# Linear attention into a gated MLP: the first k tile loaded uncast, slot 5 transposed by DMA

## The chip, the cores and the metric

The kernel runs on one core of a Trainium2 chip. The core has TensorE (PE: matmuls; its weight loads are listed apart as PEld), VectorE (DVE), ScalarE (ACT), GpSimd (POOL) and SyncE (SP). DMAs are issued by SP, ACT or POOL and carried out by 16 DMA engines. The metric is device time in microseconds; all times in this text are microseconds unless marked otherwise. Data sits in SBUF (128 partitions) and matmuls write to PSUM, which has eight banks of 128 x 512 float32.

## What is computed

The first half is a recurrence over time with a decay per head, the second half an MLP with h * cos(h):

```python
# q, k, v: (4, 8, 768, 64) float32; w_in (512, 2048), w_out (2048, 512)
gamma = 1.0 - 2.0 ** (-5.0 - np.arange(H))
scale = 1.0 / np.sqrt(D)
for t in range(S):
    state = gamma[None, :, None, None] * state + einsum('bhd,bhe->bhde', k[:, :, t], v[:, :, t])
    y[:, :, t] = scale * einsum('bhd,bhde->bhe', q[:, :, t], state)
x = y.transpose(0, 2, 1, 3).reshape(B * S, H * D)     # 3072 x 512
h = x @ w_in
out = (h * cos(h)) @ w_out                            # 3072 x 512, float32
```

## The kernel before, in words

**Slots and groups.** Time is cut into six chunks of 128 steps. A slot is one chunk of two batches (all eight heads): 12 slots, numbered in the order of `ORDER` (slots 0 and 1 are the first chunks of both batch pairs). Two slots make one group of 512 tokens for the MLP: six groups.

**A slot's attention.** q and k come in as float32 tiles `qf`, `kf`, are cast to bf16 (`qs`, `ks`; q times the decay from slot 2 on), and are transposed into `qkt`. In slots 0 and 1 the transposes are `tq`, `tk` (per half `u`), later `t`: PE transposes by a matmul against the identity (line 364) into a bank, and DVE or ACT copy the bank to `qkt` (`eq`, `ek`). From slot `DMA_T` on, two transposing DMAs per slot, issued by SP (line 353; `dt60` is q of slot 6, `dt61` its k), write `qkt` directly. Then come the scores (`a`, lines 392 and 402), their masks on DVE (`m`, line 411; two of slots 0 and 1 are split into a copy by ACT, `ms`, and a product by POOL, `ml`), and the output block `y` (lines 483 and 497) with the state update (`s`, line 511). From slot 4 on, `y` of a slot holds the scores of the next slot as well (`y4` computes the scores of slot 5), so it takes six banks. `yc` copies y to `xt` (the MLP's x), `sc` copies the state to bf16. v is cast to `vr` in slots 0 and 1 (`rv`) and scaled to `vs` (`cv`); `cq`, `ck` are the casts of q and k. The last digit is the half.

**The MLP.** `h2.6` is w_in's columns of f tiles 6 and 7 times the half group of slot 2 (line 614, eight matmuls of 256 columns); `f0.13` is f tile 13 times a full group (line 593, four matmuls of 512 columns). ACT computes the cosine of the bank (`cos...`, line 601) and DVE the product into `gt` (`mul...`, lines 605 and 622). `o2.3` is the last quarter of the second matmul for 128 tokens (line 638, four matmuls); when four quarters are done, ACT copies the bank (`oc2`) and SP stores it (line 650).

**What sets the order.** Up to slot 5 the order of every engine is decided by `Plan`, a list scheduler that runs when the kernel is built: each operation has engines that may do it, a cost, what it waits for, a rank, and tokens that it takes (banks, cosine buffers, the port that DVE and POOL share). `SHIFT` adds a number to each rank and `ON` narrows the engines; both are tables of fitted numbers. The plan decides order only; waits on the chip are semaphores for data and buffers. An engine carries out its list in order, so an operation that waits holds up all behind it. Where PE has nothing to do before 18 us, the plan puts in idle matmuls on zeros (`fill`, line 667), behind seven that stand ahead of it. Seven banks go round in a fixed order; one PSUM bank holds the state. After the plan a plain loop writes the rest: per step one `f` and one `o` unit, and a `y` block every eighth step; its first `o` unit is the one of group 1.

**Loads.** POOL issues a fixed list, in which the first load is k of slot 0 (line 284, into bf16 `ks`, so the DMA casts), then:

```python
LOADS = ["Q1", "K1", "v0", "v1", "w0A", "w0B", "w0b", "w1a", "w1b", "w2", "q2", "k2", "w3a", "v2", "w3b", "o0",
         "q3", "k3", "v3", "o1", "q4", "o2", "k4", "v4", "q5", "k5", "o3", "v5", "q6", "k6", "v6", "q7", "k7", "v7"]
```

A capital Q or K is a load that casts; q, k, v load float32 tiles; w and o are parts of w_in and w_out (they cast too; `o0` to `o3` are quarters of w_out). q of slot 0 is loaded by SP, and SP loads all slots from 8 on. SP's list is: q of slot 0, five small copies (`sw`), then stores, transposing DMAs and later loads.

Of the kernel before, what the change touches and what calls it, by code (L numbers as in the profile page):

```python
# [28 lines left out]
class Plan:  # L29
# [35 lines left out]
    def run(self, start, cold_until=0.0, look=0.0, fill=None, hold=""):  # L65
# [6 lines left out]
        t = 0.0  # L72
        while left:
            nxt = []
            for e in "SPADE":
                if free[e] > t:
                    nxt.append(free[e])
                    continue
                best = None
                soon = 1e9  # L80
                coming = []
                for op in left:
                    if e not in op["engines"]:
                        continue
                    r = self.ready(op)
                    if r is None:
                        continue
                    if r > t + 1e-9:
                        nxt.append(r)
                        coming.append((r, op["rank"]))  # L90
                        if op["rank"] < 20:
                            soon = min(soon, r)
                        continue
                    ok = True
                    for k, n in op["take"]:
                        tk = sorted(self.tokens[k])
                        n += op["spare"] if k == "bank" else 0
                        if len(tk) < n:
                            ok = False
                            continue  # L100

                        at = max(tk[n - 1] - 0.5, tk[n - 3]) if n > 5 else tk[n - 1]
                        if at > t + 1e-9:
                            nxt.append(at)
                            ok = False
                    if not ok:
                        continue
                    key = (op["rank"] + (0.5 if op["mode"] and op["mode"] != mode[0] else 0), op["n"])
                    if best is None or key < best[0]:
                        best = (key, op)  # L110
                if e == "E" and best and best[0][0] >= 1000 and soon < t + look:
                    best = None
                if e in hold and best:
                    c = best[1]["cost"]
                    c = c[e] if isinstance(c, dict) else c
                    c = c[0] if isinstance(c, tuple) else c
                    if any(r < t + 0.7 * c and k < best[0][0] - 8 for r, k in coming):
                        best = None
                if best is None:
                    if (e == "E" and fill and fill[0] <= t < fill[1] and soon > t + fill[2]  # L120
                            and min(self.tokens["bank"] or [1e9]) <= t):
                        self.add("E", fill[2], fill[3], (), 0, (), (), "full", name="fill")
                        self.ops[-1].update(eng=e, start=t, free=t + fill[2], done=t + fill[2],
                                            lat=0.0)
                        free[e] = t + fill[2]
                        mode[0] = "full"
                        nxt.append(free[e])
                    continue
                op = best[1]
                left.remove(op)  # L130
                c = op["cost"][e] if isinstance(op["cost"], dict) else op["cost"]
                busy, took = c if isinstance(c, tuple) else (c, c)
                if e == "E":
                    if t < cold_until:
                        busy, took = 2 * busy, 2 * took
                    if op["mode"] != mode[0]:
                        busy, took = busy + self.SWITCH, took + self.SWITCH
                        mode[0] = op["mode"]
                for k, n in op["take"]:
                    self.tokens[k].sort()  # L140
                    del self.tokens[k][:n]
                op.update(eng=e, start=t, free=t + busy, done=t + took, lat=self.LAT[e])
                free[e] = t + busy
                if op["mb"]:
                    self.dma = max(self.dma, t + busy + 1.6) + op["mb"] / op["rate"] + op["lag"]
                    op.update(done=self.dma + 0.9, lat=0.0)
                for k, n in op["give"]:
                    self.tokens[k] += [op["done"] + 0.052] * n
                nxt.append(free[e])
                nxt.append(op["done"] + op["lat"])  # L150
            later = [x for x in nxt if x > t + 1e-9]
            if left and not later:
                raise RuntimeError("the plan is stuck at %s: %s" % (t, [o["name"] for o in left][:9]))
            t = min(later) if later else t
# [12 lines left out]
HOLD = ""  # L167
# [6 lines left out]
def kernel(  # L174
# [170 lines left out]
    def conv_k(p, b, e):  # L345
        copy(e, kb(p)[:, b], kf[p % PRE][:, b])
# [654 lines left out]
```

## Time and profile before

| | |
|---|---|
| time, median of 3 runs (lowest to highest) | 208.82 (208.31 to 208.92) |
| span of the profiled execution, first to last instruction | 206.6 |
| the profiled execution's own time | not recorded beside its span; the median is 2.2 above the span |
| PE busy | 201.9 (98%), 2179 matmuls |
| DVE, ACT, POOL busy | 112.9, 115.1, 75.2 |
| chain that ended last | PE 93%, DMA 4% |
| granted TensorE clock | full (1.000) |

The page of the profile lists the busy time of each engine, the span in 40 slices (each digit is a busy share in tenths), the chain of work that ended last, and groups of instructions. The trace behind it answers questions: a timeline (start, length, engine, line, operation, output<-input, count), who waited for whom, and from which issue a DMA landed when. "Landing" is the time from issue to arrival. Landings used below are issue plus that time: k of slot 0 at 7.7, Q1 9.4, K1 11.3, v0 13.0, o0 32.6, k6 57.3, k7 61.8, v7 63.3.

### The profile page before, as it was taken

What the parts mean: (1) busy time and instruction counts of PE and PEld (TensorE: products, weight loads), DVE (VectorE), ACT (ScalarE), POOL (GpSimd) and SP (SyncE); (2) the same over time, 40 slices, a digit from 0 to 9 for tenths busy, and PEclk for the clock granted to TensorE, in tenths of its full rate; (3) what the DMA queues carried; (4) which work ended last, traced back from release to release, by engine and by line L of the source; (5) the groups of instructions that cost most, each with busy time, mean ns of one, the idle gap of its engine ahead of it and who ended that gap; (6) DMA issues with size and microseconds to landing.
All of it is one profiled execution on the core that took longest, in us unless ns stands there. A gap on an engine that the chain in (4) does not pass through costs nothing.

```text
span 206.6 us, 5235 instructions
## 1 busy us (share of the span) xinstructions
PE 201.9 (98%) x2179; PEld 108.9 (53%) x2179; DVE 112.9 (55%) x194; ACT 115.1 (56%) x193; POOL 75.2 (36%) x79
## 2 busy tenths in 40 slices
PE   7999999999999999999999999999999999999994
PEld 2547665868945545445445445445444444444442
DVE  5477899776787548338438438448442444444000
ACT  7566794859965357547547546554555553554120
POOL 8899989799985003305206105200000000000000
PEclk9999999999999999999999999999999999999999
DMA  6999999999999865886876975501101101110212
GB/s 117 172 264 201 304 242 322 252 333 278 341 332 190 199 156 150 206 210 155 190 183 157 144 198 147 156 0 56 53 1 51 51 3 51 51 51 0 105 52 102
DMA packets 59656, 32.15 MB, mean 156 GB/s; under 512 B 48752, under 2 KB 54128, under 8 KB 59632
## 3 DMA queue, kind: packets, MB, share of 16 engines
q0 software_dynamic: 15408, 15.47, 34.6%
q1 hardware_dynamic: 44080, 16.28, 31.7%
q8 instruction: 17, 0.28, 0.6%
q10 hardware_dynamic: 144, 0.07, 0.1%
q14 instruction: 7, 0.06, 0.1%
HBM read 27.26 MB, written 6.29 MB: 162 GB/s over the span
## 4 chain that ended last, share of the span: by engine, by line
PE 93%; DMA 4%; POOL 1%; issue 0%; DVE 0%; POOLq 0%; DVEq 0%
PE bank L638 39%; PE bank L593 30%; PE bank L614 10%; DMA kx<-in_k_dram 4%; PE bank L392 2%; PE bank L483 2%; PE bank L364 2%; PE bank L658 2%; PE st_ps L511 2%; PE bank L667 2%; PE bank L497 1%; POOL ks L284 1%; PE bank L434 1%; POOL qs L284 1%; PE bank L402 0%
## 5 line engine op out<-in xcount | busy, mean ns | idle before, releaser
L601 ACT ACTIVATE cosb<-bank,halfpi 128x512 bf16<-128x512 f32 x96 | 65.6, 689 | 54.1 <-PE bank L593 47.8
L638 PE MATMUL bank<-w_out_sb,gt 128*128 128x512 bf16 x368 | 91.0, 379 | 0.0
L605 DVE TENSOR_TENSOR gt<-bank,cosb 128x512 bf16<-128x512 f32 x72 | 49.1, 689 | 55.7 <-ACT cosb L601 55.7
L593 PE MATMUL bank<-xt,w_in_sb 128*128 128x512 bf16 x288 | 73.2, 379 | 0.0
L638 PEld LDWEIGHTS <-gt 128*128 128x128 bf16 x368 | 35.5, 98 | 42.3 <-DMA w_out_sb<-in_moe_w_out_dram 0.3
L593 PEld LDWEIGHTS <-w_in_sb 128*128 128x128 bf16 x288 | 27.5, 98 | 32.3
L327 POOL TENSOR_TENSOR qs<-qf,gq 128x512 bf16<-128x512 f32 x18 | 18.5, 1046 | 42.4 <-PE bank L483 32.0
L411 DVE TENSOR_TENSOR am<-bank,mask 128x512 bf16<-128x512 f32 x40 | 24.8, 681 | 3.5 <-PE bank L392 3.5
L316 ACT COPY ob<-bank 128x512 f32<-128x512 f32 (+1 forms) x24 | 14.0, 582 | 16.0 <-PE bank L638 13.9
L614 PE MATMUL bank<-xt,w_in_sb 128*128 128x256 bf16 x192 | 22.4, 273 | 0.0
L614 PEld LDWEIGHTS <-w_in_sb 128*128 128x128 bf16 x192 | 18.6, 98 | 3.3 <-DVE xt L318 0.3
L622 DVE TENSOR_TENSOR gt<-bank,cosb 128x512 bf16<-128x512 f32 x24 | 16.2, 689 | 5.6 <-ACT cosb L601 5.4
L316 ACT CAST xt<-bank 128x512 bf16<-128x512 f32 x21 | 11.4, 588 | 10.6 <-PE bank L483 10.5
L316 ACT CAST ks<-kf 128x512 bf16<-128x512 f32 x20 | 11.5, 623 | 1.9 <-DMA kf<-in_k_dram 1.9
L667 PE MATMUL bank<-zero 128*128 128x512 bf16 x35 | 11.2, 449 | 1.1 <-DVE halfpi L683 1.1
L483 PE MATMUL bank<-am,vs 64*64 64x128 bf16 (+1 forms) x320 | 10.3, 206 | 0.1
L334 POOL TENSOR_TENSOR vs<-vf,gk 128x512 bf16<-128x512 f32 x8 | 8.2, 1043 | 6.0 <-DMA vf<-in_v_dram 3.8
L284 POOL DMA_DIRECT2D vf<-in_v_dram x8 | 9.4, 1178 | 1.9 <-DVE vs L339 1.4
L339 POOL TENSOR_TENSOR vs<-vf,gk 128x512 bf16<-128x512 f32 x8 | 8.7, 1096 | 2.5 <-PE bank L483 1.3
L318 DVE CAST stb<-st_ps 128x512 bf16<-128x512 f32 x9 | 6.2, 689 | 3.4 <-PE st_ps L511 2.6
L483 PEld LDWEIGHTS <-vs 64*64 64x64 bf16 x320 | 7.8, 107 | 0.5 <-POOLq L531 0.2
L392 PE MATMUL bank<-qkt 64*64 64x128 bf16 (+1 forms) x320 | 7.9, 206 | 0.0
(66 smaller groups left out, 131.7 us busy)
## 6 DMA issues: line engine op xcount, KB each, us to landing
out_dram<-ob SPq DMA_DIRECT2D x23, 256.0 KB, 2.5
vf<-in_v_dram POOLq DMA_DIRECT2D x8, 512.0 KB, 11.7
qf<-in_q_dram POOLq DMA_DIRECT2D x6, 512.0 KB, 12.3
kf<-in_k_dram POOLq DMA_DIRECT2D x6, 512.0 KB, 12.1
w_out_sb<-in_moe_w_out_dram POOLq DMA_DIRECT2D x4, 512.0 KB, 14.1
qf<-in_q_dram SPq DMA_DIRECT2D x4, 512.0 KB, 4.8
w_in_sb<-in_moe_w_in_dram POOLq DMA_DIRECT2D x5, 256.0 KB, 8.5
kf<-in_k_dram SPq DMA_DIRECT2D x16, 64.0 KB, 3.1
```

Of the source, the lines that this page charges most:

```text
L284: eng.dma_start(out=t.rearrange("p b h d -> p (b h) d"), in_=src[ds(2 * bp, 2), :, ds(c * C, C), :].rearrange("b h t d -> t (b h) d"))
L316: nc.scalar.copy(out=out, in_=in_)
L327: ENG[e].tensor_tensor(out=qb(p)[:, b], in0=qf[p % PRE][:, b], in1=bc(gq, ORDER[p] % NC), op=ALU.mult)
L411: nc.vector.tensor_tensor(out=am[p % 2][b][u], in0=bank.rearrange("p (a t) -> p a t", a=HP), in1=(dec[:, b] if p < 2 else mask[second(p, 0 ...
L483: m = nc.tensor.matmul(held["yp", p][b][ts(j, 64), a, lo:], lhsT=vs[p % NB][ts(r, 64), b, h, :], rhs=am[p % 2][b][h // 4][ts(r, 64), h % 4 ...
L593: nc.tensor.matmul(bank, lhsT=w_in_sb[:, i, ts(f, 128)], rhs=xt[g % 2][:, i, :], start=(i == 0), stop=(i == KIN - 1))
L601: nc.scalar.activation(out=cb, in_=bank, func=AF.Sin, bias=halfpi)
L605: nc.vector.tensor_tensor(out=gt[g % 2][:, f, :], in0=bank, in1=cb, op=ALU.mult)
L614: nc.tensor.matmul(bank[:, ts(e, 256)], lhsT=w_in_sb[:, i, ts(f + e, 128)], rhs=xt[g % 2][:, i, ts(hf, 256)], start=(i == 0 and e == 0), s ...
L622: nc.vector.tensor_tensor(out=gt[g % 2][:, f : f + 2, ts(hf, 256)], in0=bank.rearrange("p (f t) -> p f t", f=2), in1=cb.rearrange("p (f t) ...
L638: nc.tensor.matmul(bank, lhsT=gt[g % 2][:, f, ts(j, 128)], rhs=w_out_sb[:, f, :], start=(f == 0), stop=(f == KOUT - 1))
L667: nc.tensor.matmul(bank[:, : 256 * n].rearrange("p (n t) -> p n t", n=n), lhsT=zero[:, :128], rhs=zero.unsqueeze(1).to_broadcast([128, n, ...
```

## The change

k of slot 0 is loaded as float32 into `kf` (`"K"` becomes `"k"`) and cast to `ks` by two new operations `ck00`, `ck01`; `ON` gives them to ACT. q of slot 0 (`cq00`, `cq01`) was cast on DVE and is cast on POOL and ACT. `DMA_T` goes from 6 to 5: slot 5's transposes `t50`, `t51` and its four copies out of the bank leave PE, ACT and DVE, and `dt50`, `dt51` are issued by SP, without the plan's condition that k of slot 7 has landed. The plan's assumed load rates, lags and start times change, its rule for the port, and all entries of `SHIFT` and `ON`. The order that comes out:

- PE, start: 18 idle matmuls ahead of `tq00` (7 before); then `tq01 tk01 tk00 tq10 tq11 a01 a00 tk11 tk10 a11 a10 y01 y00 y10 y11 h0.0 h0.2 h1.2 h1.0 s0 h1.4 h1.6 h0.6` with idle matmuls between. Before, `h0.0` stood ahead of `y10 y11`. From there to the first `o` unit the same kinds of units.
- PE, around slots 4 and 5, before: `y3 t41 t40 h2.6 h3.0 h3.2 h3.8 h3.4 h3.6 h3.12 h3.10 t50 t51 h3.14 o1.3 a4 o0.2 o2.0 o0.3 o2.1 y4 o2.2 o3.0 o2.3 o3.1 o3.2 y5 o3.3`, then the loop. After: `y3 t41 t40 o0.0 h3.8 h3.4 h3.10 o0.1 h3.14 o0.2 o1.3 a4 o0.3 h3.6 h3.0 h3.12 o2.2 o3.0 o2.3 o3.1 y4 o3.2 o3.3 h3.2 y5`, then the loop.
- ACT, start, after: `cq01 eq00 ck01 ck00 ek01 ms011 ek11 rv01 rv00 ms111 rv10 rv11`, then cosines. Around slot 4, after: `oc1 ck61 oc0 ck60 cosh3.6 cosh3.0 cosh3.12 oc2 sc4 yc40 yc41 ck70 ck71 oc3 cosh3.2 yc51 yc50 sc5`.
- DVE, start, after: `eq01 ek00 eq10 eq11 m001 m010 ek10 m000 m101 m100 m110 yc01 yc00 yc10 cv01 yc11 cv11 mulh0.0`. Around slot 4, after: `m411 m401 m400 m410 mulh3.6 cv60 mulh3.0 mulh3.12 cv51 m511 m501 m510 m500 mulh3.2`.
- POOL: the loads in the same order; `cq00` stands between K1 and v0; `cv41` and `cq50` change places.
- SP, after: `dt51 dt50`, store of `oc1`, store of `oc0`, `dt60`, store of `oc2`, `dt61 dt70`, store of `oc3`, `dt71`. Before: two stores, `dt61 dt60 dt70 dt71`, two stores.

```diff
--- before.py
+++ after.py
@@ -93,6 +93,8 @@
                         continue
                     ok = True
                     for k, n in op["take"]:
+                        if k == "port" and e == "A":
+                            continue
                         tk = sorted(self.tokens[k])
                         n += op["spare"] if k == "bank" else 0
                         if len(tk) < n:
@@ -137,6 +139,8 @@
                         busy, took = busy + self.SWITCH, took + self.SWITCH
                         mode[0] = op["mode"]
                 for k, n in op["take"]:
+                    if k == "port" and e == "A":
+                        continue
                     self.tokens[k].sort()
                     del self.tokens[k][:n]
                 op.update(eng=e, start=t, free=t + busy, done=t + took, lat=self.LAT[e])
@@ -144,7 +148,11 @@
                 if op["mb"]:
                     self.dma = max(self.dma, t + busy + 1.6) + op["mb"] / op["rate"] + op["lag"]
                     op.update(done=self.dma + 0.9, lat=0.0)
+                elif op["lag"]:
+                    self.dma = max(self.dma, t + busy) + op["lag"]
                 for k, n in op["give"]:
+                    if k == "port" and e == "A":
+                        continue
                     self.tokens[k] += [op["done"] + 0.052] * n
                 nxt.append(free[e])
                 nxt.append(op["done"] + op["lat"])
@@ -165,8 +173,8 @@
 
 
 HOLD = ""
...
+ON = {"cq00": "P", "ck00": "A", "cv00": "D", "rv00": "A", "cq01": "A", "ck01": "A", "cv01": "D", "eq00": "A", "sc0": "D", "yc00": "D", "yc01": "D", "rv10": "A", "cv11": "D", "rv11": "A", "eq10": "D", "ek10": "D", "eq11": "D", "yc10": "D", "yc11": "D", "cq20": "D", "cv20": "P", "cq21": "D", "cv21": "P", "eq20": "D", "ek20": "D", "eq21": "A", "sc2": "A", "yc20": "D", "cv30": "D", "cv31": "D", "eq30": "D", "ek30": "D", "eq31": "A", "ek31": "D", "sc3": "A", "yc31": "DA", "eq40": "A", "ek40": "D", "cv51": "D", "yc50": "DA", "cv60": "D"}
 HALF0, SPARE, RF, RM, COLD = 8, 1, 50.0, 50.0, 5.2
 
 
@@ -194,7 +202,7 @@
     NG = NP // 2
     PRE = 5
     NB = 3
-    DMA_T = 6
+    DMA_T = 5
 
     ORDER = [0, NC] + [x for x in range(1, NP) if x != NC]
     SWAP = 8
@@ -677,7 +685,7 @@
     nc.gpsimd.iota(far[:, 8:24], pattern=[[1, 16]], base=0, channel_multiplier=0,
                    allow_small_or_imprecise_dtypes=True)
     load(nc.sync, 0, "q0 q1")
-    load(nc.gpsimd, 0, "K")
+    load(nc.gpsimd, 0, "k")
     nc.vector.memset(zero, 0.0)
     nc.vector.memset(lnsc, math.log(scale))
     nc.vector.memset(halfpi, math.pi / 2.0)
@@ -710,24 +718,25 @@
     CQ, CD = "P", "DP"
     SPLIT = {(1, 1, 1), (0, 1, 1)}
     HM, HCQ, HCV = "q2", "", ""
-    plan = Plan({"bank": 7, "cos": 3, "sem": 8, "out": 4, "port": 1, "ring": 7}, 6.5)
+    plan = Plan({"bank": 7, "cos": 3, "sem": 8, "out": 4, "port": 1, "ring": 7}, 6.33)
     add = plan.add
     SB2 = {"D": (0.33, 0.42), "A": (0.49, 0.585)}
+    SB3 = dict(SB2, P=(1.0, 1.02))
     TT = {"D": (0.6, 0.69), "P": (1.03, 1.05)}
     PS = {"D": (0.6, 0.69), "A": (0.49, 0.585)}
     ld = {}
     prev = None
     at = lambda tm: dict(start=0.0, free=0.0, done=tm, lat=0.0)
-    ld["q", 0, 0], ld["q", 0, 1], ld["k", 0, 0], ld["k", 0, 1] = map(at, (3.9, 5.0, 7.4, 7.4))
+    ld["q", 0, 0], ld["q", 0, 1], ld["k", 0, 0], ld["k", 0, 1] = map(at, (3.85, 4.8, 7.25, 7.25))
     LOADS = ["Q1", "K1", "v0", "v1", "w0A", "w0B", "w0b", "w1a", "w1b", "w2", "q2", "k2", "w3a", "v2", "w3b", "o0", "q3", "k3", "v3", "o1", "q4", "o2", "k4", "v4", "q5", "k5", "o3", "v5", "q6", "k6", "v6", "q7", "k7", "v7"]
-    LAG = {"w1b": 0.15}
+    LAG = {"w1a": 0.45, "w3b": -0.15, "v2": 0.15, "o1": 0.6}
     pend = []
     for i, x in enumerate(LOADS):
         if x[0] in "qkvQK":
             p = int(x[1:])
             o = add("P", 1.2, lambda e, p=p, n=x[0]: load(nc.gpsimd, p, n),
                     [("issued", prev)] if prev else [], 50 + i if p < 7 else 45,
-                    [("sem", 1), ("ring", 1)], [("sem", 1), ("ring", 1)], mb=524288e-6, rate=330e-3, name=x)
+                    [("sem", 1), ("ring", 1)], [("sem", 1), ("ring", 1)], mb=524288e-6, rate=(300e-3 if x[0] in "QK" else 335e-3 if i < 9 else 345e-3), lag=LAG.get(x, 0.0), name=x)
             ld[x[0].lower(), p, 0] = ld[x[0].lower(), p, 1] = o
             if p >= PRE:
                 pend.append((o, x[0], p - PRE))
@@ -736,14 +745,14 @@
             lo += 512 * int(x[1])
             o = add("P", 0.76, lambda e, lo=lo, n=n: load_w_in(lo, n),
                     [("issued", prev)], 50 + i, [("sem", 1)], [("sem", 1)],
-                    mb=n * 2048e-6, rate=(415e-3 if n > 256 else 390e-3 if n > 128 else 370e-3),
+                    mb=n * 2048e-6, rate=(412e-3 if n > 256 else 400e-3 if n > 128 else 385e-3),
                     lag=LAG.get(x, 0.0), name=x)
             for f in range(lo // 128, (lo + n) // 128):
                 ld["w", f] = o
         else:
             r = int(x[1])
             o = add("P", 0.76, lambda e, r=r: load_w_out(r), [("issued", prev)], 50 + i,
-                    [("sem", 1)], [("sem", 1)], mb=1048576e-6, rate=415e-3, name=x)
+                    [("sem", 1)], [("sem", 1)], mb=1048576e-6, rate=420e-3, lag=LAG.get(x, 0.0), name=x)
             ld["o", r] = o
         prev = o
     T = {}
@@ -752,27 +761,28 @@
         c = ORDER[p] % NC
 
         for b in range(2):
-            if p == 1:
-                T["cq", p, b], T["ck", p, b] = ld["q", p, b], ld["k", p, b]
+            if p == 1 and "Q1" in LOADS:
+                T["cq", p, b] = ld["q", p, b]
             else:
-                T["cq", p, b] = add("D" if p < 2 else CQ if p < 3 else "P", SB2 if p < 2 else TT,
+                T["cq", p, b] = add("DAP" if p < 2 else CQ if p < 3 else "P", SB3 if p < 2 else TT,
                                     lambda e, p=p, b=b: conv_q(p, b, e),
                                     [ld["q", p, b], G("tq", p - NB, b), G("dt", p - NB, 0)],
                                     10 * p + b, [("port", 1)], [("port", 1)], name="cq%d%d" % (p, b))
-            if p == 0:
+            if p == 1 and "K1" in LOADS:
                 T["ck", p, b] = ld["k", p, b]
-            elif p > 1:
-                T["ck", p, b] = add("A", SB2, lambda e, p=p, b=b: conv_k(p, b, e),
-                                    [ld["k", p, b], G("tk", p - NB, b), G("dt", p - NB, 1), G("s", p - NB)],
-                                    10 * p + b, name="ck%d%d" % (p, b))
+            else:
+                T["ck", p, b] = add("DAP" if p < 2 else "A", SB3, lambda e, p=p, b=b: conv_k(p, b, e),
+                                    [ld["k", p, b], G("tk", p - NB, b), G("dt", p - NB, 1),
+                                     G("s", p - NB)],
+                                    10 * p + b, [("port", 1)], [("port", 1)], name="ck%d%d" % (p, b))
             cd = add(CD if p == 2 else "P", TT, lambda e, p=p, b=b: conv_v(p, b, e),
                      [ld["v", p, b], G("y", p - NB, b), G("s", p - NB)],
                      10 * p + 1.5 + b + (20 if p == 0 else 60 if p == 1 else 0),
                      [("port", 1)], [("port", 1)], name="cv%d%d" % (p, b))
             T["cd", p, b] = T["cv", p, b] = cd
             if p < 2:
-                T["cv", p, b] = add("AD"[b], SB2, lambda e, p=p, b=b: raw_v(p, b, e), [ld["v", p, b]],
-                                    10 * p + 2.5 + b, [("port", 1)] if b else [], [("port", 1)] if b else [],
+                T["cv", p, b] = add("AD", SB2, lambda e, p=p, b=b: raw_v(p, b, e), [ld["v", p, b]],
+                                    10 * p + 2.5 + b, [("port", 1)], [("port", 1)],
                                     name="rv%d%d" % (p, b))
         old = [G("a", p - NB, b) for b in range(2)] + [G("y", p - NB, b) for b in range(2)]
         if p < DMA_T:
@@ -799,9 +809,11 @@
             kq = {u: [T["eq", p, u], T["ek", p, u]] for u in range(2)}
         else:
             for w, x in enumerate("qk"):
-                T["dt", p, w] = add("S", (1.3, 4.6), lambda e, p=p, w=w: dma_t(p, w),
-                                    [T["c" + x, p, 0], T["c" + x, p, 1], ld["k", 7, 0]] + old, 10 * p,
-                                    name="dt%d%d" % (p, w))
+                T["dt", p, w] = add("S", (1.3, 5.6 if p < 6 else 4.6),
+                                    lambda e, p=p, w=w: dma_t(p, w),
+                                    [T["c" + x, p, 0], T["c" + x, p, 1],
+                                     ld["k", 7, 0] if p > 5 else None] + old, 10 * p,
+                                    lag=1.1 if p < 6 else 0.0, name="dt%d%d" % (p, w))
             kq = {u: [T["dt", p, 0], T["dt", p, 1]] for u in range(2)}
         if p > PL:
             continue
@@ -859,7 +871,7 @@
         for b in range(2):
             done = [G("h", p2, f) for p2 in (p - 4,) for f in range(0, 16, 2)] if p >= 4 else []
             done += [G("f", (p - 4) // 2, f) for f in range(16)] if p >= 4 else []
-            T["yc", p, b] = add("A", PS, lambda e, p=p, b=b: y_copy(p, b, e),
+            T["yc", p, b] = add("DA" if p < 2 else "A", PS, lambda e, p=p, b=b: y_copy(p, b, e),
                                 [T["y", p, b]] + done, 10 * p + 5, (), [("bank", 1)],
                                 name="yc%d%d" % (p, b))
 
@@ -917,7 +929,7 @@
         add("A", (0.49, 0.585), lambda e, j=j: (o_out(0, j, e), o_dma(0, j)), [T["o", j, 3]], 300, (),
             [("bank", 1)], name="oc%d" % j)
     plan.shift(SHIFT, ON)
-    plan.run({"S": 2.5, "P": 3.2, "A": 5.5, "D": 3.6, "E": 4.2}, COLD, 0.6, (4.2, 18.0, 0.225, lambda e: idle_mm(e, 2)), HOLD)
+    plan.run({"S": 2.5, "P": 3.2, "A": 6.6, "D": 3.6, "E": 4.2}, COLD, 0.6, (4.2, 18.0, 0.225, lambda e: idle_mm(e, 2)), HOLD)
     plan.emit()
```

## The prediction

> **What bounds the kernel now.** I read the page first (engine shares, the 40 slices, the chain that ended last), then the waits of TensorE, then the timelines of the stretches that the change touches.
>
> ```profile
> span 206.6 us, 5235 instructions
> PE 201.9 (98%) x2179; PEld 108.9 (53%) x2179; DVE 112.9 (55%) x194; ACT 115.1 (56%) x193; POOL 75.2 (36%) x79
> PE   7999999999999999999999999999999999999994
> PE 93%; DMA 4%; POOL 1%; issue 0%; DVE 0%; POOLq 0%; DVEq 0%
> ```
>
> TensorE (PE) is busy in every slice, and the chain is PE for 93%. The first 16 us of that are mostly idle matmuls on zeros. From 18.85 us on, the timeline of PE shows each group starting where the one before stopped, so a microsecond of matmuls taken away is a microsecond gained, as long as no new wait opens. In that dense part the waits table names one load that is only just in time, the first quarter of w_out (o0):
>
> ```profile
> PEld L638 <- DMA w_out_sb<-in_moe_w_out_dram: 0.3, 1, 0.3
> ```
>
> Its first matmul starts at 32.65, straight behind the f units (30.91 + 8 x 0.216 = 32.64); only the weight load stood 0.3 us for it. So PE and the load queue arrive together at 32.6.
>
> The timelines of PE, ACT and SP around the edits (start, length, then the operation):
>
> ```profile
> 55.38 0.39 PE L364 MATMUL bank<-ident,qs 128*128 128x128 bf16 x4
> 55.61 0.39 PE L364 MATMUL bank<-ident,ks 128*128 128x128 bf16 x4
> 55.83 0.39 PE L364 MATMUL bank<-ident,qs 128*128 128x128 bf16 x4
> 56.05 0.39 PE L364 MATMUL bank<-ident,ks 128*128 128x128 bf16 x4
> 56.28 1.04 PE L614 MATMUL bank<-xt,w_in_sb 128*128 128x256 bf16 x8
> ```
> ```profile
> 62.56 1.33 SPq L353 DMA_TRANSPOSE qkt<-ks  x1
> 64.07 3.37 SPq L353 DMA_TRANSPOSE qkt<-qs  x2
> 67.55 1.24 SPq L353 DMA_TRANSPOSE qkt<-ks  x1
> ```
> ```profile
> DMA to landing us min/median/max: 2.7/2.8/4.4
> 131.00:132.00 1.00, 1.00 (x7) 0.42 (x5) 0.19 (x1) 0.73 (x2) 0.00 (x0) 1.00 0.76 168
> ```
> The first fence is slot 5 on PE; the second the transposing DMAs of slots 6 and 7; in the third, the first line says that those land 2.7 to 4.4 us after issue, and the second (a stretch with nothing but the tail of two such DMAs) ends with the busy share of the 16 DMA engines, 0.76, and 168 GB/s.
>
> **The change part by part**, against this execution: span 206.6, and 208.82 - 206.6 = 2.2 us around it, since the median timed run is 208.82 (its own time is not recorded).
>
> **1. Slot 5 off PE.** Sixteen transposes go: 56.28 - 55.38 = **0.90 us** of dense PE time (the same group took 0.89 at 28.42 and at 40.17). Its four copies to qkt (two on ACT of 0.59, two on DVE of 0.42) go too, worth nothing: both engines are idle over 40%.
>
> **2. What takes their place.** SP issues dt51 (k) and dt50 (q) ahead of the first output store. dt50 waits for the second half of slot 5's q on POOL, at 53.11 + 2.05 = 55.2 (POOL does the same work before it in either order). Block y4 reads the result: before it started at 62.23; now PE has done 0.90 less of transposes, one h unit less (h3.2, 0.87) and four o units more (56 matmuls of w_out instead of 40, 3.46), so 63.92, with the first read 0.38 into it (62.61 - 62.23): 64.3. From 55.2 that is 9.1 us against 2.7 to 4.4 measured: hidden.
>
> Whose cover is thinner is the load queue behind them. A transposing DMA takes about 0.76 x 262 KB / 168 KB = 1.18 us of all 16 engines. If the loads give way fully, two cost later loads 2.36 us; the lower end is nothing, for the 256 KB store issued at 59.58 left the landings of q7 and k7 1.5 us apart as before. I take 1.9, since dt50 starts late for k6. Loads v5 to v7 are late next. k6 (issued 45.18, 12.1 to landing: 57.3) matters most: on ACT its cast ck61 now stands ahead of oc0, ck60 and three cosines; DVE has four operations behind these, the last of which frees the bank that y4's first a-matmul takes. From landing: 0.54 + 0.48 + 0.54 (pitch of casts and copies) + 0.69 (cosine) + 0.06 + 3 x 0.60 + 0.68 + 0.06 = 4.85, so 62.15, needed at 64.3: **2.15 us of cover**. Lag 1.9 costs 0; 2.36 costs 0.2; beyond that, a microsecond each. The other late loads have more (k7 lands at 61.8, its cast is due after y4, at 66.9).
>
> The Trainium skill, DMA: Bandwidth & Descriptors, "Issuing engines are not separate DMA queues", says that DMAs of all issuers share the same 16 engines and interleave, which speaks against this edit. Its transposing rate of 261 GB/s would make each 1.0 us (an estimate from that page), the lag 2.0 and the cost nothing; no row of this trace has transposes beside a full load queue.
>
> **3. SP's new order.** Slot 6's k transpose (dt61) stood behind the second store; it now stands behind the third, which waits for o2.3 on PE and oc2 on ACT: o2.3 ends at 63.92 - 0.86 = 63.06, oc2 at 63.9, the store issues in 0.5, dt61 goes at 64.4 and lands at 67.1 to 68.8. y5 reads it at 68.11 + 0.37 = 68.5 (y5's start comes in part 4): cost 0 to 0.3; I take 0, since 2.8 is the median.
>
> **4. Behind y4.** y4 (1.49) ends at 65.41. Then two o units (1.83), h3.2 (0.87), y5 at 68.11, ending at 69.59 (68.14 to 69.62 before, 1.48). Before, o3.3 followed and covered the emptying of banks; now the loop's first o unit comes at once and needs the bank of h3.2. ACT from y4's end: sc4, yc40, yc41 (0.48 each), ck70, ck71 (0.54 each), oc3 (0.48), then the cosine of h3.2 (0.69), its product on DVE (0.04 + 0.68 + 0.06). Starting 0.1 behind y4 that is 4.57, so 69.98, a wait of 0.39; if sc4 starts 0.2 before y4's end (its sums are ready then), 0.09. I take **0.2**. The loop's first o unit then starts at 69.8; before, at 69.62 + 0.87 = 70.49. So parts 1 to 4 gain **0.7** (0.5 to 0.8).
>
> **5. The start.** k of slot 0 needs no cast in the DMA but two on ACT, behind cq01 and eq00; cq00 goes to POOL. POOL then issues v0 about 1.0 later (nearest row: a POOL product of 1.05; no copy on POOL is in the trace; from 0.6, ACT's cast, to 1.3, the longest POOL product, all hidden): v0's packets wait for the loads ahead anyway (landings 9.39, 11.33, 12.97, 14.6). Eighteen idle matmuls now stand ahead of the first transpose. The granted clock reads full in all slices, but the pace of the idle matmuls doubles: cold they come every (3.17 - 0.63) / 6 = 0.42 us, warm every (1.69 - 0.38) / 6 = 0.22; before, the pace changed at about 6.2. So 12 cold and 6 warm: 1.06 + 5.04 + 1.32 = 7.4. Then eq00, ck01, ck00 on ACT (0.2 + 0.48 + 0.54 + 0.61) and tk00: 9.3 to 9.6, where slot 0's k was transposed from 7.80 before. DVE works from about 10.0 without a gap worth counting: three qkt copies (0.35), two masks (0.60), a copy, four masks, yc01, yc00: 10.0 + 4 x 0.35 + 8 x 0.60 + 0.1 = 16.3; h0.0 starts at 16.4 (15.75 before), and h1.2, after yc10, cv01, yc11, at 18.2 to 18.5 (18.85 before). From h1.2 to the first o unit PE has the same work as before plus s0 (0.4): 32.65 - 18.85 + 0.4 = 14.2, so 32.4 to 32.7. Against 32.65: **0**, between -0.3 (o0 lands earlier: k's first issue took 1.37 where uncast ones take 1.18, and two cast loads landed 1.94 apart where uncast ones land 1.63) and +0.4 (the clock opens 0.8 later).
>
> By the Trainium skill, TensorE: Matmul & The Clock Gate, Part 1, about 3.4 us of sustained work open the clock, which here took 5.1. By that rule the idle matmuls would end at 6.6 (an estimate from that page) and o1.0 would be held by o0's landing alone, -0.2.
>
> **6. Moves** of h, o, mask and copy operations between engines and places change no PE work; ACT and DVE keep idle time. From the loop on, order and work are as before.
>
> Sum: -0.90 + 0.2 + 0 (start) = -0.7: span 205.9, time **208.1**. A run can tell about 0.3% (0.63 us) from no change, so this is just past the line.
>
> **The rivals.** (a) *The start or dt61 eats it*: clock late (+0.4) or dt61 at 68.8 (+0.3), or both: 208.4 to 208.8. For: both places have under 0.4 us of slack; against: median landing 2.8. (b) *Slower*: the two transposes hold the load queue longer than 1.18 each, so that k6's cast blocks ACT and y4 waits. It costs from lag 2.15 on and turns the sign at 2.15 + 0.7 = 2.85, 1.4 us per transpose. At the isolated landing of 2.8 each the lag is 5.6: +3.4 - 0.7 = +2.7, 211.5; at 1.8 each, +0.7, 209.5. For: loads land back to back, 1.5 us apart, until v7 at 63.3; against: the store's row, and that the second one starts when k6 is nearly through. (c) *More*: o0 and the start both early by 0.3, the wait of part 4 at 0.1: 207.7. (d) *Nothing moves*, because PE has as many transposes: excluded, the instruction order shows sixteen fewer on PE and two more on SP.
>
> **How the numbers follow.** Forecast 207.9 to 208.3: 0.43; (c) 0.12; (a) 0.20; (b) 0.20; slower for a cause that I have not named: 0.05. Faster by over 0.3% (below 208.19): three quarters of the forecast (0.32) and all of (c): 0.44. Within: the rest of the forecast (0.11), (a), and a fifth of (b) (0.04): 0.35. Slower (above 209.45): the rest of (b) and the unnamed: 0.21. Range: from (c) less 0.2 for runs, 207.5, to (b) at its middle price, 209.6; outside it 1 in 10 below and above each. The likeliest case's own range is 207.9 to 208.3.
>
> **What would show it.** Right: PE group L364 short by 16 records around 55 us and no PE idle from 18.5 to 70 above 0.4 us in all; the first o unit at 32.4 to 32.7; y4 at 63.9, y5 at 68.1; dt50 landed before 61. Wrong: the first o unit later than 33 (part 5); landings of k6 above 59.5 with ck61 idle on DMA, and y4 later than 64.3 (part 2, rival b); a wait on the DMA of qkt in y5 (part 3); more than 0.4 idle before the loop's first o unit (part 4).

## The result: 1.6% slower, a wait inside y4

The changed kernel took 212.34 us (median of 6 runs, 211.01 to 213.07), the kernel before 208.87 (6 runs, 208.31 to 209.98): ratio 1.0159, 95% interval 1.0127 to 1.0190. Forecast were 208.1, and 207.5 to 209.6. The profiled execution took 212.0 with a span of 210.2.

The page of the changed kernel shows where, in its 40 slices of 5.26 us:

```profile
span 210.2 us, 5183 instructions
...
PE   7999999999995999999999999999999999999993
...
PEclk9999999999998899999999999999999999999999
```

PE was gap-free before; now one slice (63 to 68 us) is half empty, and in it and the next the granted clock falls. The waits of PE between 18 and 90 us (line waited for: total, times, longest) name the cause in the first row:

```profile
PE bank L400 <- DMA qkt<-qs: 2.3, 1, 2.3
PE bank L646 <- issue: 0.7, 3, 0.3
PE bank L646 <- DVE gt L630: 0.2, 1, 0.2
```

L400 is the product of k and q of slot 5, which y4 carries along; it waits for dt50, the transposing DMA of slot 5's q. SP's own timeline (start, duration) shows dt50 being issued at 54.8, 0.4 earlier than forecast (55.2), but with an issue of 5.96 us where the other transposing DMAs take 1.3 to 2.6:

```profile
51.10 1.34 SPq L361 DMA_TRANSPOSE qkt<-ks  x1
54.82 5.96 SPq L361 DMA_TRANSPOSE qkt<-qs  x1
60.87 1.00 SPq L658 DMA_DIRECT2D out_dram<-ob  x2
```

and the chain of work that ended last gives its landing, 54.82 + 11.87 = 66.7:

```profile
54.82 11.87 DMA qkt<-qs
66.69 0.14 issue
66.83 0.26 PE bank L400
```

The first one, dt51, landed 13.2 after its issue, at 64.3. Both had been given 2.7 to 4.4. Why they took so long stands in the DMA packets. In the changed kernel from 57 to 61 us, queue by queue (packets, MB, share of 16 engines):

```profile
q0 software_dynamic: 345, 1.27, 94.5%
q1 hardware_dynamic: 349, 0.09, 10.6%
```

The software queue's loads (q0) and the transposes (q1) move packet for packet, 345 against 349. But a packet of a load is mostly 4 KB (1.27 MB in 345 packets) and one of a transpose 256 bytes (0.09 MB in 349). So the transposes got 87 packets per us; the two of them have 2048. In the kernel before, with no load beside them, the same kind of DMA moved 1693 packets in the 2 us from 64 to 66:

```profile
q1 hardware_dynamic: 1693, 0.43, 104.1%
```

The Trainium skill, DMA: Bandwidth & Descriptors, "Queues, rings and completion order", says that each DMA engine goes round its queues packet by packet; these counts agree with it. The forecast had not used that rule.

Turns are not the whole of the 11.9 us. Counted in short windows, no packet of the transposes moves before 55.25, although dt51 was issued at 51.10. From 55 to 61, beside the loads, 446 of the 2048 go. By 64.70 all 2048 are gone: from there to 65.85 the hardware queue moves 237 packets, and only 17 of them are under 512 bytes (the rest are those of the output stores). Yet dt50 counts as landed only at 66.7, 2.0 later. What holds it at the two ends, before the first packet and after the last, no run here separates.

The loads, which the forecast had expected to pay, hardly gave way: the software queue's last packet came at 63.5 instead of 62.9, and ck61, the cast of slot 6's k, started at 57.36, where the forecast's sum without any lag has it (57.3).

After the wait PE ran at half clock. Four stretches of 3.41 us of the changed kernel (length, busy time of PE, instructions, granted clock, DMA share, GB/s):

```profile
59.57:62.98 3.41, 3.41 (x22) 1.00 1.19 279
62.98:66.39 3.41, 1.53 (x43) 1.00 1.55 273
66.39:69.81 3.42, 2.65 (x76) 0.50 0.84 217
69.81:73.22 3.41, 3.41 (x125) 1.00 0.46 125
```

The stretch with the pause has PE busy for 45%; the one after it runs at 0.50. The timed runs show the same: five of the six have a mean clock of 0.991 or 0.992 and took 212.0 to 213.07, the sixth kept 0.999 and took 211.01.

### The profile page after: what moved, and what is told of

It reads as the page before. It is cut to its first block, busy times and chain, and to the rows that moved or that the text cites. A ratio compares the mean times of both kernels' runs of the same rounds, so it can differ in the third digit from the quotient of the medians.

```text
span 210.2 us, 5183 instructions
## 1 busy us (share of the span) xinstructions
PE 201.0 (96%) x2142; PEld 109.2 (52%) x2166; DVE 113.4 (54%) x193; ACT 115.0 (55%) x191; POOL 75.3 (36%) x80
## 2 busy tenths in 40 slices
DMA packets 59848, 32.93 MB, mean 157 GB/s; under 512 B 48816, under 2 KB 54192, under 8 KB 59824
## 3 DMA queue, kind: packets, MB, share of 16 engines
HBM read 27.26 MB, written 6.29 MB: 160 GB/s over the span
## 4 chain that ended last, share of the span: by engine, by line
PE 66%; DMA 19%; POOL 10%; issue 2%; ACT 1%; DVE 0%; POOLq 0%; DVEq 0%
PE bank L646 33%; PE bank L601 26%; DMA vf<-in_v_dram 7%; DMA w_out_sb<-in_moe_w_out_dram 6%; DMA qkt<-qs 6%; POOL kf L292 2%; PE bank L666 2%; PE bank L400 2%; POOL qf L292 2%; PE bank L491 2%; POOL vf L292 1%; PE st_ps L519 1%; POOL w_in_sb L311 1%; POOL qs L335 1%; PE bank L505 1%
## 5 line engine op out<-in xcount | busy, mean ns | idle before, releaser
L601 PE MATMUL bank<-xt,w_in_sb 128*128 128x512 bf16 x274 | 71.3, 380 | 0.6 <-issue 0.2
L601 PEld LDWEIGHTS <-w_in_sb 128*128 128x128 bf16 x288 | 27.5, 98 | 32.4 <-issue 0.2
L324 ACT CAST ks<-kf 128x512 bf16<-128x512 f32 x22 | 12.8, 626 | 1.8 <-DMA kf<-in_k_dram 1.8
L324 ACT CAST xt<-bank 128x512 bf16<-128x512 f32 x18 | 9.8, 590 | 6.8 <-PE bank L491 5.3
L675 PE MATMUL bank<-zero 128*128 128x512 bf16 x38 | 12.0, 442 | 1.2 <-DVE halfpi L691 1.1
L491 PE MATMUL bank<-am,vs 64*64 64x128 bf16 (+1 forms) x320 | 11.0, 212 | 0.1
L400 PE MATMUL bank<-qkt 64*64 64x128 bf16 (+1 forms) x320 | 8.6, 213 | 2.3 <-DMA qkt<-qs 2.3
L400 PEld LDWEIGHTS <-qkt 64*64 64x64 bf16 x320 | 7.3, 112 | 3.8 <-issue 2.9
L491 PEld LDWEIGHTS <-vs 64*64 64x64 bf16 x320 | 8.4, 110 | 0.5 <-POOLq L539 0.2
```

The costliest lines, as they stand in the source:

```text
L324: nc.scalar.copy(out=out, in_=in_)
L400: return nc.tensor.matmul(ap[b][ts(x, 64), a, lo:], lhsT=kt(p % NB, b, h)[:, ts(x, 64)], rhs=qt(p % NB, b, h)[:, lo:], tile_position=(64 * ...
L491: m = nc.tensor.matmul(held["yp", p][b][ts(j, 64), a, lo:], lhsT=vs[p % NB][ts(r, 64), b, h, :], rhs=am[p % 2][b][h // 4][ts(r, 64), h % 4 ...
L601: nc.tensor.matmul(bank, lhsT=w_in_sb[:, i, ts(f, 128)], rhs=xt[g % 2][:, i, :], start=(i == 0), stop=(i == KIN - 1))
```

## The experiments

In all of them the planner's choice of place and engine for every operation is written out as a list, in the order in which the operations are emitted, and only the entries named below move. P, A, D, E, S are POOL, ACT, DVE, PE and SP. The ratios are against runs of the kernel before on the same chip, which showed medians of 209.03 (e1 to e4), 209.28 (e5 to e8) and 209.07 (e9 to e11).

The first question is between two theories: the loss is slot 5's wait and the half clock behind it, or it is the start and the many moves that came with the new order. If it is the first, there are again two: the transposes take turns with the loads packet by packet, or beside the loads they take a fixed time of some 12 us from their issue.

### e1: slot 5 back on PE, the rest of the change kept

```diff
-    DMA_T = 5
+    DMA_T = 6
 order: - dt51:S, dt50:S
        + t50:E t51:E after h3.12; eq50:A eq51:A after cosh3.12; ek50:D ek51:D after mulh3.12
```

> The changed kernel with its order written out and kept, but slot 5 transposed on PE again (sixteen transposes right after h3.12, four copies out of their banks), so that all else of the change stays: k of slot 0 uncast, every move. If the loss is the wait of y4 for slot 5's transposes, the pause of 2.3 us in y4 and the half clock of 3.4 us behind it (worth about 1.4) go and 0.9 of PE work comes back: 212.3 - 2.3 - 1.4 + 0.9 = 209.5, between 208.8 and 209.6, y5 at 69.0. If the moves or the start lost the time, it stays above 211.

Measured: 209.21 (10 runs), ratio 1.0013 (0.9995 to 1.0030). No wait for a DMA of qkt, clock 1.0, y5 at 69.37. So everything in the change except slot 5 makes no difference that can be measured (at most 0.3%, by the interval), and slot 5 is the loss.

### e2: only slot 5, in the kernel before

```diff
-    DMA_T = 6
+    DMA_T = 5
 order: - t50 t51 eq50 eq51 ek50 ek51
        + dt51:S after ck50 and v7's issue; dt50:S after cq51
```

> The kernel before with its order written out and kept, and slot 5 alone moved from PE to two DMA transposes, issued behind ck50 and cq51 as in the changed kernel. PE then reaches y4 0.9 earlier, at 61.3. If transposes beside the loads take turns with them packet by packet (in the changed kernel 57 to 61 us: 78, 95, 88, 84 packets of the loads and 77, 95, 88, 89 of the transposes in each us), slot 5's 2048 packets end near 66.7 whatever PE does, so y4 pauses some 4.9 us: -0.9 + 4.9 + 1.4 for the half clock = +5.4, 214.3 (213.3 to 215.3). If the moves or the start lost the time, slot 5 alone gains 0.9: 208.0.

Measured: 211.25, ratio 1.0103 (1.0080 to 1.0126), the ratio from three runs at 211.2 to 211.3. A fourth took 215.5; its mean granted clock was 0.981 where the three show 1.000, so it lost clock, but it was not profiled. The sign and the mechanism are the first theory's, the size is 3 us short of it. The waits of PE:

```profile
PE bank L427 <- DMA qkt<-qs: 2.7, 1, 2.7
PE bank L649 <- DMA w_in_sb<-in_moe_w_in_dram: 1.0, 1, 1.0
```

dt50 landed at 54.63 + 10.5 = 65.1 instead of 66.7, so the pause was 2.7 and not 4.9, and the half clock never came. (The two transposes' last packet goes at 64.5, in the changed kernel at 64.7; the 1.6 us between the landings lie behind it and are not explained.) The stretches (here with all engines: PE, PEld, DVE, ACT, POOL, then clock, DMA share, GB/s) show why that can be:

```profile
60.04:63.45 3.41, 2.34 (x47) 1.05 (x45) 1.26 (x3) 0.59 (x1) 2.04 (x2) 1.00 1.18 240
63.45:66.87 3.42, 1.75 (x77) 1.43 (x78) 1.01 (x2) 0.54 (x2) 0.59 (x1) 1.00 1.39 272
66.87:70.28 3.41, 3.41 (x17) 1.57 (x16) 2.68 (x5) 2.16 (x5) 1.59 (x2) 1.00 0.94 207
```

The 2.7 us of pause fell across two stretches, so that PE was busy for 69% and 51% of them, and the clock stayed. In the changed kernel a shorter pause fell almost whole into one.

### e3: the transposes issued 6 to 9 us later

```diff
 order: - dt51:S (after cosh3.8), dt50:S (after cv50)
        + dt51:S dt50:S after oc0
```

> The changed kernel with its order written out and kept, but the two transposes of slot 5 are issued behind the first two stores, about 59.3 and 60.8 instead of 51.1 and 54.8. If packets take turns, the 4 to 8 us issued earlier were worth only some 700 of 2048 packets, which run in under 1 us once the loads are over at 62.5: landing at 66 to 67.5, time 211.5 to 213.5. If a transpose beside loads takes a fixed 12 us from its issue, it lands near 72, y4 pauses 7.5: 217.

Measured: 213.11, ratio 1.0198 (1.0169 to 1.0227): the landing is no fixed time from the issue, and the time is in the range given for turns. That the queues take turns is read from the packet counts above. SP and PE in the timeline of e3:

```profile
59.83 1.37 SPq L396 DMA_TRANSPOSE qkt<-ks  x1
61.31 2.57 SPq L396 DMA_TRANSPOSE qkt<-qs  x1
...
67.44 0.22 PE L435 MATMUL bank<-qkt 64*64 64x128 bf16 x2 [2.11 <-DMA qkt<-qs]
```

The two landed at 59.83 + 6.5 = 66.3 and 61.31 + 6.0 = 67.3: issued 8.7 and 6.5 us later than in the changed kernel, they came 2.0 and 0.6 later. The early issue had bought 0.6 us for dt50.

### e4: slot 7's loads out of the software queue

```diff
-lambda e, p=p, n=x[0]: load(nc.gpsimd, p, n)
+lambda e, p=p, n=x[0]: load(nc.sync if e == "S" else nc.gpsimd, p, n)
 order: - q7:P k7:P v7:P, dt50:S (after cv50), dt60:S dt61:S (around o3.1)
        + dt50:S after cq51, dt60:S after cq61, dt61:S k7:S q7:S v7:S after ck60
```

> The changed kernel with its order written out and kept, but the three loads of slot 7 leave the software queue and are issued by SP, behind the transposes of slots 5 and 6, which now follow one another. The software queue ends with v6 at 58.8. If packets take turns, slot 5's transposes then run at the full rate from 58.8 and land by 61.5, slot 6's by 65, y4 does not pause, y5 starts at 68.1, and the time is the 208.1 that was forecast (207.7 to 208.8; up to 209.5 if slot 7's k lands after 69 and holds ACT). If a transpose takes a fixed 12 us from its issue, slot 5's lands at 63.3, and slot 6's at 70, which pauses y5 by 2: 210 to 211.5.

Measured: 209.25 (10 runs, 208.41 to 210.57), ratio 1.0014 (0.9989 to 1.0039). SP:

```profile
53.47 4.76 SPq L396 DMA_TRANSPOSE qkt<-qs  x1
58.32 0.54 SPq L693 DMA_DIRECT2D out_dram<-ob  x1
59.04 1.31 SPq L396 DMA_TRANSPOSE qkt<-qs  x1
```

The software queue's last packet is at 57.9; slot 5's q landed at 53.47 + 7.3 = 60.8, slot 6's q, issued at 59.04 with no load beside it, after 3.0. y4 does not wait. The wait is thus the loads' doing. dt50's issue still took 4.76 us; SP's next issue, at 58.32, came when the loads were over. The time is 1.1 above the forecast of 208.1 all the same. Its waits on PE:

```profile
PE bank L657 <- DMA w_in_sb<-in_moe_w_in_dram: 0.7, 1, 0.7
PE bank L681 <- DVE gt L665: 0.6, 1, 0.6
```

The first is at the start (the first o unit at 33.54, against 32.63 in the profile of the changed kernel), the second in front of the loop, where ACT stood 0.78 for slot 7's k.

### e5: only k of slot 5 by DMA

```diff
-(t_mm(p, u, 0), t_mm(p, u, 1))
+(t_mm(p, u, 0), p == 5 or t_mm(p, u, 1))
 def t_copy(p, u, w, e):
+    if p == 5 and w == 1:
+        return dma_t(5, 1) if u == 0 else None
...
-        if w == 1:
+        if w == 1 or p == 5:
             banks.give(bank)
```

> The changed kernel with its order written out and kept, but only k of slot 5 is transposed by DMA (issued at 51.1 as in the changed kernel); q of slot 5 is transposed by PE, eight transposes (0.45 us) right after h3.12 with two copies. If packets take turns, 1024 instead of 2048 packets fit beside the loads: the first of the changed kernel's two transposes landed at 64.3, and y4 reaches slot 5 0.45 later than there, at 64.9, so no wait and no half clock; half of the 0.9 is kept: 209.2 (slot 5 all on PE) - 0.45 = 208.8, between 208.3 and 209.3. If one transpose beside the loads is as late as two, landing at 66 or later, PE pauses and the time is above 210.5.

Measured: 209.42, ratio 1.0018 (1.0001 to 1.0035); y5 at 69.15. The transpose landed at 51.71 + 12.5 = 64.2, and PE did not wait, as expected if half the packets fit beside the loads. From the first o unit to y5 it took 35.91, 0.45 less than e1 (36.36), as expected. The total, against e1's 1.0013, does not show it: 0.45 us is less than the intervals.

### e6: the pause filled with idle matmuls

```diff
         h, lo = 4 * u + a, 64 * second(p, x, b, u)
+        if p == 5 and not held.get("warm"):
+            held["warm"] = True
+            for i in range(9):
+                nc.tensor.matmul(held["a", 5, 0][0], lhsT=zero[:, :128], ...)
```

> The changed kernel with its order written out and kept, plus nine idle matmuls of 128x512 on PE (0.216 each, 1.9 us) ahead of the first product of slot 5 in y4, where PE stands 2.3 us in the changed kernel. The wait for the DMA stays, what is left of it 0.2 to 0.6. If the half clock behind the pause is a cost of its own, it is gone: y4 to y5 takes 8.07 - 1.45 = 6.6 instead of 8.07, time 212.3 - 1.45 = 210.9 (210.3 to 211.4), mean clock 1.0. If the slow stretch after the pause came from late DVE and ACT work, the time stays at 212.3.

Measured: 211.39, ratio 1.0106 (1.0080 to 1.0132), 0.5% or 1.1 us below the changed kernel's 1.0159. The clock stayed (same columns as for e2):

```profile
64.72:68.14 3.42, 3.42 (x103) 1.88 (x102) 0.00 (x0) 0.03 (x1) 0.00 (x0) 1.00 1.18 236
68.14:71.55 3.41, 3.25 (x74) 2.10 (x66) 2.48 (x4) 3.04 (x7) 2.04 (x2) 1.00 1.03 260
```

From the first product of slot 5 to y5 it took 71.33 - 67.52 = 3.81, in the changed kernel 71.98 - 66.84 = 5.14. The half clock is a cost of its own, 1.3 us, on top of the 2.3 of the wait; the whole time is lower by 1.1.

### e8: the kernel before, once more

No edit; only the order is a list.

> The kernel before with its order written out and nothing changed, as a measure of what two builds and two profiles of the same work differ by: 208.9 (208.3 to 209.5), ratio 1.000. Its first o unit tells whether the start of these runs is later than in the first profile of the kernel before (32.65): 33.0 to 33.5 if that is the chip or chance, 32.65 if the later starts of e1, e3 and e4 belong to the change.

Measured: 209.31, ratio 1.0002 (0.9986 to 1.0019). Its first o unit was at 34.15, 1.5 later than in the first profile of the same work, with 1.1 of it in one wait:

```profile
PE bank L649 <- DMA w_in_sb<-in_moe_w_in_dram: 1.1, 1, 1.1
```

Late starts are thus no mark of the change. From the first o unit to the end both profiles of the kernel before take 173.95 (206.6 - 32.65 and 208.1 - 34.15); that stretch is the better scale for what follows.

### e7, e9 and e10: the e4 kernel without its wait in front of the loop

e7 moves only ck70 and ck71 behind cosh3.2 on ACT; e9 moves dt71 behind them as well; e10 also moves h3.2 ahead of o3.3 on PE. Against e4:

```diff
 e9 order:  - ck70:A ck71:A (after yc41), dt71:S (after oc3)
            + ck70:A ck71:A dt71:S after cosh3.2
 e10 order: - h3.2:E (after o3.3), cosh3.2:A
            + h3.2:E after yc40, cosh3.2:A after yc41
```

> The kernel with slot 7's loads behind the transposes (e4_slot7_behind), with one move: on ACT ck70 and ck71, which there waited 0.78 for slot 7's k and held cosh3.2 and with it the loop's first o unit by 0.57, come after cosh3.2. If that was what the forecast's 0.7 went into, 209.25 - 0.57 = 208.7 (208.2 to 209.2), and 208.3 where the start loses nothing. If e4's missing gain lies in the start (first o unit at 33.5 there, 32.6 in the changed kernel), it stays near 209.2.

> The kernel with slot 7's loads behind the transposes (e4_slot7_behind), with ck70 and ck71 moved behind cosh3.2 on ACT and the transpose of slot 7's k behind them on SP. In e4 ACT stood 0.78 for slot 7's k and held cosh3.2, and the loop's first o unit stood 0.57. If that wait is what e4 still lost, y5 to the end takes 138.1 instead of 138.69 and the ratio falls from 1.0014 to 0.9987 (0.996 to 1.001): about 208.8 where the kernel before shows 209.1. If the loss lies elsewhere, the ratio stays at 1.001 to 1.003.

> e9_slot7_casts with one more move: on PE h3.2 comes before o3.3 and on ACT cosh3.2 before oc3, so that the product of h3.2 is no longer what the loop's first o unit waits for (0.24 in the changed kernel). Expected 0.2 below e9: ratio 0.998 (0.9955 to 1.0005), about 208.6. If bank or DVE order costs as much as it gains, the same as e9.

e7 left dt71 ahead of the casts, in the list and so in the program: it transposes the tile before slot 7's k is in it, and the casts have to wait for it. PE stood 8.4 us behind ACT, and the time was 219.0; it tells nothing of the question.

e9: 209.39, ratio 1.0014 (0.9988 to 1.0039). The wait in front of the loop fell from 0.6 to 0.23, but the total did not: y5 to the end took 138.7 as in e4, with the missing time in the loop's first 40 us (PE busy for 39.5 of them, 40.0 in the kernel before); 0.18 of it is a wait for a transposing DMA of a later block at 109.5; the rest I have not found. The expected gain did not come.

e10: 209.09 (12 runs, 208.12 to 210.49), ratio 1.0001 (0.9978 to 1.0024), and 206.4 - 32.85 = 173.55 from the first o unit to the end in its profile. That is 0.4 below the kernel before, and no difference in the time that can be measured. None of the versions beats the kernel before.

### e11: k of slot 0 cast by its load again, slot 5 on PE

```diff
-    load(nc.gpsimd, 0, "k")
+    load(nc.gpsimd, 0, "K")
 order: e1's, without ck00 and ck01
```

> The kernel with slot 5 back on PE (e1_slot5_pe), with one thing more undone: k of slot 0 is cast by its load again and ck00 and ck01 are left out, so that tk00 need not wait for ACT but for a load that lands about 7.7. If the start is worth nothing either way, as was forecast, the time is e1's: ratio 1.001 (0.998 to 1.004), first o unit between 32.6 and 33.7 as in the seven starts measured so far. If the uncast load gained at the start, this is slower than e1 by 0.3 to 0.8 (ratio 1.003 to 1.005); if it lost, faster by as much.

Measured: 209.12, ratio 1.0003 (0.9986 to 1.0021), first o unit at 32.93. The uncast load of slot 0's k is worth nothing that can be measured, either way.

## Why the prediction was wrong

Times and stretches of each profile, in us. y4 and y5 are counted from the first matmul in them that reads the bf16 state (the tile `stb`).

| kernel | first o unit | y4 | y5 | span | first o to y5 | y5 to end |
|---|---|---|---|---|---|---|
| before | 32.65 | 62.24 | 68.14 | 206.6 | 35.49 | 138.5 |
| before again (e8) | 34.15 | 63.74 | 69.65 | 208.1 | 35.50 | 138.5 |
| forecast | 32.65 | 63.92 | 68.11 | 205.9 | 35.46 | 137.8 |
| changed | 32.63 | 63.91 | 71.98 | 210.2 | 39.35 | 138.2 |
| e1, slot 5 on PE | 33.01 | 65.18 | 69.37 | 207.4 | 36.36 | 138.0 |
| e4, loads moved | 33.54 | 64.82 | 69.01 | 207.7 | 35.47 | 138.7 |

**Part 1, slot 5 off PE: right.** e1 less e4 is 36.36 - 35.47 = 0.89 for sixteen transposes, and e5 shows half of it.

**Part 2 failed, and it is the whole result.** Its sentence was that dt50, from 55.2, had 9.1 us against 2.7 to 4.4 measured: hidden. Those 2.7 to 4.4 were measured when the loads had ended or were ending, and I carried them to a place where the loads were still running. Beside them the landing took 11.9 to 13.2, and y4 waited 2.3. The same part then took the load queue to be the one whose cover was thin, and gave it a lag of 1.9; the loads gave way by about 0.6 and the transposes paid. I had divided the engines' time by the bytes; what is divided is turns. The rows for it were at hand. Of the kernel before, from 57 to 60:

```profile
q0 software_dynamic: 283, 1.03, 102.9%
```

That is about 94 turns per us. 2048 packets of 256 bytes (262 KB of a transpose by 1024) need 22 us of that, and between the issue at 51.1 and the end of the loads at 63 there are 12. So dt50 could not land before the loads were over. Turns do not give the whole wait, though. Counted from the first packet at 55.25, 7.75 x 94 = 728 packets go by 63, and the other 1320, at the 847 per us measured without loads, are through at 64.6; the last one was seen at 64.7. But the landing came 2.0 behind that packet, where e2 and e3 show 0.6 and 0.7. So about 1.3 of y4's 2.3 is a delay at the very end, whose cause stays open.

**The half clock** stood in no part, since no wait was forecast. It cost 1.3. Together: 208.1 + 2.3 + 1.3 = 211.7; with the 0.4 by which y5 to the end is longer than forecast, 212.1, where 212.34 was measured.

**Part 3, dt61: cost 0, as taken.** With y4 on time (e1, e5) it landed at 65.48 + 3.3 = 68.8 and 65.24 + 4.0 = 69.2, before y5 began or just after, and y5 did not wait. **Part 4, the wait behind y4: right**, 0.24 where 0.2 was taken.

**Part 5, the start: right in size, in part by luck.** In brackets the forecast: the first o unit at 32.63 (32.4 to 32.7), 18 idle matmuls to 7.0 (7.4), h0.0 at 16.5 (16.4). The idle matmuls ended earlier because the clock opened at 4.95, 3.9 after the first of them, where part 5 had carried over 5.1. And the start varies from profile to profile far more than my range for it: 32.6 to 33.7 with the new order, 32.65 to 34.15 with the old.

**Part 6, moves: nearly free.** The stretch from y5 to the end is 0.2 to 0.4 longer than forecast in the kernels that keep the order behind y5 (138.0 to 138.2); what it is I have not separated.

**The rivals.** (b) had the right sign and prices of 209.5 to 211.5, short of 212.3; its mechanism, k6 landing late and holding ACT, did not happen. Of the signs listed for being right, y4 at 63.9 and the first o unit came; "dt50 landed before 61", no more than 0.4 of idle PE and y5 at 68.1 failed, and the wait on the DMA of qkt that was listed for y5 came in y4. And without the wait the forecast of 208.1, a ratio of 0.9966, would not have come either: e4, e9 and e10, where y4 does not wait, show 1.0001 to 1.0014. Part of this shows in the profile of e1: with slot 5 on PE it takes 207.4 - 33.01 = 174.4 from the first o unit to the end, 0.4 more than the kernel before, so the new order takes back about half of the 0.9 that slot 5 gives. e10, at 173.55, is 0.4 below the kernel before.

## What to carry to other kernels

How long a DMA takes to land depends on what runs beside it, so a landing measured alone can't be carried to a place where a load stream runs. Here a transfer in small packets beside a stream of large ones got as many packets as the stream, not as many bytes: count its packets, divide by the stream's packets per us, and expect the rest to go through only when the stream ends. Issuing it earlier bought 0.6 us (e3); taking loads out of the stream (e4), or putting half the transfer elsewhere (e5), ended the wait. A wait of PE can have a half clock behind it, which here cost more than half of the wait itself; price it as well where the wait fills over half of a clock window.

## What the runs showed of the hardware that was not expected

The second of two transposing DMAs beside the loads also held up SP, which issues it: dt50's issue took 5.96 us in the changed kernel, 6.03 in e2 and 4.76 in e4, against 1.3 for one with nothing beside it. So the first store, whose data was ready at 57.0, went out at 60.87. What the issue waits for is not shown; in the changed kernel it ended at 60.78, before the first transpose had landed (64.3).

The granted clock changed in steps of a fixed window. In the changed kernel it opened at 4.95 (the pace of the idle matmuls doubles) and fell at 66.39, in e3 it opened at 6.29 and fell at 67.73: 61.44 in both, 18 times 3.413. The low stretch behind lasted 3.41 in both, and in e7, behind the wait of 8.4, twice that, from 76.0 to 82.8. A window with PE busy for 45% was followed by a low one, as was one with 38% (e3); one with 51% was not (e2). Between these the limit is not measured. The Trainium skill, TensorE: Matmul & The Clock Gate, Part 1, gives the same free-running window of about 3.4 us, but lets the clock fall after an idle window; here it fell after windows that were only about half idle. So a wait of 2 to 3 us cost 1.3 more (the changed kernel) or nothing (e2), by where it fell.
